# First pair's k ahead of q and turned in two halves, double score steps from the start, and a new order of all tasks

## The chip, the cores and the metric

The kernel runs on one core of a Trainium2 chip. The metric is the device time of one execution in microseconds (us); smaller is better. "Faster" and "slower" mean by more than 0.3% here, which is about what a measurement of this kernel can tell from no change.

The engines are TensorE (PE; its weight loads are shown apart as PEld), VectorE (DVE), ScalarE (ACT), GpSimd (POOL) and SyncE (SP, which only issues DMAs). DMAs are also issued by ACT and by POOL.

## The reference

A thresholded attention of 8 batches with 8 heads, 576 rows and head size 64, and behind it a mixer over all heads of a batch:

```
scores = q @ k.T / 8                                # 576 x 576 for each head
thresh = max(scores, axis=-1) - tau                 # tau = 0.02
scores = where(scores >= thresh, scores, -1e9)
attn   = softmax(scores)
x      = attn @ v                                   # heads side by side: 576 x 512 for each batch
u      = x + ((x.T @ U) @ V).T                      # rank 32
out    = u + relu(u @ w_ch1) @ w_ch2                # 512 -> 2048 -> 512
```

## The kernel before

**Pairs, steps and tiles.** Two heads of a batch make a pair: 32 pairs, numbered 0 to 31. 576 rows are four and a half times 128, so two neighbouring pairs share a tile: for them there are nine steps of 128 rows (four of each pair's own, one in which each pair has half of the rows), 144 steps in all, counted from 0 below. Each step has two score tiles of 128x576, one for each head.

**One pair on its way.** `load_tasks` brings q and k from HBM into `qkraw` (two buffers, pair p uses buffer p % 2) in eight DMAs: for each of the two heads, q and k, and the lower and the upper 64 partitions. `prepare_tasks` turns them on PE against an identity matrix (L568: four 128x128 turns for q and four for k, L581: one for the ninth tile of both) and ACT copies the results from PSUM to `qkT` (L574, L587). `score_tasks` multiplies q and k (L637, 16 matmuls for a step, in fp32) into the PSUM tiles `trio0` and `trio1`. Then, for each score tile, DVE scales, negates and takes the row minimum (`weigh`, L666), ACT computes the threshold of a step (L682) and the exponential (L689), and DVE selects and sums (`select`, L696, into `w_ring`). The weights are turned by DMA (L720) or, for some tiles of the first eight pairs, by PE and ACT (`turn_pe` L727, `copy_w` L737). `value_tasks` multiplies with v (L796, L804, later L800), normalises, and does the low-rank part; `mixer_tasks` does the two big products of a finished batch (L994 and L1010, L1027).

**Single and double steps.** A score task does one step or two at once. A double task holds both steps' scores in PSUM, so DVE has four tiles to weigh before PE must come again. The switch `LONE = 2` makes every step of pairs 0 and 1 single; from pair 2 on the first of nine is single and the other eight are done as four doubles. The next score task waits for the weighs of the two steps before it.

**The order is a table.** All work is cut into tasks. `ORDER` lists their numbers in the order in which they are emitted, found by a search ahead of time; each engine runs its own instructions in that order, and so does each DMA queue. A negative entry -n puts a filler matmul on zeros there (L469), which computes nothing and keeps PE at work; the table has 49 of them, all in the first part. `BANK` says which PSUM bank a task uses.

**Rings.** `w_ring` has four buffers: step n writes buffer n % 4, and its `select` must wait until the weights of step n - 4 have been turned.

## Time and profile before

| | us |
|---|---|
| median of 3 runs (590.59 to 592.37) | 591.26 |
| the profiled execution, its own time | 590.78 |
| its span, from the first to the last instruction | 589.0 |
| PE busy in the span | 568.7 |
| DVE busy | 509.9 |
| ACT busy | 460.2 |
| POOL busy | 331.7 |

The profiled execution is 0.48 us below the median and 1.78 us longer than its span. Busy time of PE counts fillers, and matmuls overlap, so that a PE with 9.95 us busy in 10 us has no gap. The granted clock of TensorE reads 1.00, its upper level of 2.4 GHz, in every stretch of the profile.

### The profile page before, as it was taken

The numbers are of one execution on the slowest core, as the hardware profiler recorded it, in microseconds if no ns is written. First come the engines' busy times: TensorE is split into PE (matmuls) and PEld (weight loads), VectorE is DVE, ScalarE is ACT, GpSimd is POOL, SyncE is SP. The second block draws the span as 40 slices with busy tenths as digits, with TensorE's granted clock in tenths as the row PEclk, the third lists the DMA queues.
The fourth block names the chain that finished last, engine by engine and source line by source line (L and its number), as shares of the span: only waits on it lengthen the run. The fifth ranks groups of instructions, "written<-read, shape, count | busy, mean of one in ns | idle before, by whom it ended". The sixth has DMA issues, their size and how long they took to land.

```text
span 589.0 us, 16929 instructions
## 1 busy us (share of the span) xinstructions
PE 568.7 (97%) x6142; PEld 345.8 (59%) x6214; DVE 509.9 (87%) x1400; ACT 460.2 (78%) x959; POOL 331.7 (56%) x580
## 2 busy tenths in 40 slices
PE   9898899999999999999999999999999999999996
PEld 3456655765666665555566665655665746556553
DVE  4999999999999999999998999999899799953101
ACT  4688999998899977998788987799877896774430
POOL 3887775968576748764666765566645551341000
PEclk9999999999999999999999999999999999999999
DMA  5999999969999999998989989999898798672303
GB/s 134 170 166 182 179 133 175 188 113 176 193 155 186 147 173 203 165 175 166 159 166 173 188 147 198 162 188 186 142 175 165 122 167 168 134 117 46 72 1 90
DMA packets 226996, 90.49 MB, mean 154 GB/s; under 512 B 205408, under 2 KB 217520, under 8 KB 226912
## 3 DMA queue, kind: packets, MB, share of 16 engines
q1 hardware_dynamic: 212544, 67.48, 70.5%
q0 software_dynamic: 13408, 21.58, 19.8%
q8 instruction: 49, 0.80, 0.6%
q10 hardware_dynamic: 960, 0.34, 0.2%
q14 instruction: 35, 0.29, 0.2%
HBM read 37.90 MB, written 9.44 MB: 80 GB/s over the span
## 4 chain that ended last, share of the span: by engine, by line
PE 56%; DVE 2%; issue 1%; ACT 0%
PE trio L637 13%; PE bank L1027 12%; PE trio L994 6%; PE bank L994 6%; PE trio L1027 4%; PE bank L800 4%; PE trio L800 3%; PE bank L1010 1%; PE bank L568 1%; PE trio L568 1%; DVE s_sb L666 1%; PE bank L875 1%; DVE w_ring L696 1%; PE bank L796 0%; PE trio L1010 0%
## 5 line engine op out<-in xcount | busy, mean ns | idle before, releaser
L689 ACT ACTIVATE e_sb<-s_sb,m 128x576 bf16<-128x576 f32 x288 | 217.5, 774 | 37.2 <-DVE s_sb L666 18.0
L696 DVE SCALAR_TENSOR_TENSOR w_ring<-s_sb,thr,e_sb 128x576 bf16<-128x576 f32 x288 | 229.7, 823 | 5.5 <-issue 1.5
L666 DVE TENSOR_SCALAR_CACHE_REDUCE s_sb<-trio 128x576 f32<-128x576 f32 x288 | 205.3, 749 | 9.3 <-PE trio L637 8.5
L637 PE MATMUL trio<-qkT 64*64 64x288 f32 (+2 forms) x2304 | 161.8, 410 | 2.1 <-DVE s_sb L666 1.6
L714 POOL COPY w_ring<-w_ring 128x128 bf16<-128x128 bf16 (+1 forms) x168 | 65.0, 395 | 115.3 <-DVE w_ring L696 71.7
L637 PEld LDWEIGHTS trio<-qkT 64*64 64x64 f32 x2304 | 81.4, 133 | 52.9 <-DVE s_sb L666 6.4
L1027 PE MATMUL bank<-W2b,R 128*128 128x512 bf16 x402 | 101.6, 380 | 1.9 <-issue 0.6
L506 POOL DMA_DIRECT2D qkraw<-in_k_dram x117 | 76.6, 656 | 25.9 <-PE trio L568 12.0
L1027 PEld LDWEIGHTS <-R 128*128 128x128 bf16 x576 | 53.1, 98 | 60.8 <-issue 9.1
L506 POOL DMA_DIRECT2D qkraw<-in_q_dram x117 | 76.4, 655 | 12.0 <-PE bank L581 3.0
L994 PEld LDWEIGHTS <-W1b 128*128 128x128 bf16 x512 | 46.7, 98 | 55.9 <-issue 10.9
L862 POOL TENSOR_TENSOR x<-x,rec 128x256 f32<-128x256 f32 (+1 forms) x84 | 52.7, 631 | 33.0 <-DVE x L855 21.8
L984 ACT ACTIVATE R<-bank 128x512 bf16<-128x512 f32 x80 | 47.2, 594 | 29.6 <-PE bank L994 16.4
L994 PE MATMUL bank<-uT,W1b 128*128 128x512 bf16 x244 | 66.6, 380 | 1.8 <-DVE x L855 0.2
L603 POOL TENSOR_TENSOR vh<-vraw_ring,vh 64x128 bf16<-64x128 f32 x64 | 53.5, 835 | 19.1 <-ACT vh L596 9.5
L800 PEld LDWEIGHTS <-wT_ring 128*128 128x128 bf16 x896 | 55.5, 98 | 9.9 <-issue 3.6
L994 PE MATMUL trio<-uT,W1b 128*128 128x512 bf16 x231 | 57.6, 379 | 0.4
L984 ACT ACTIVATE R<-trio 128x512 bf16<-128x512 f32 x64 | 37.5, 597 | 8.4 <-PE trio L994 8.0
L682 ACT ACTIVATE thr<-m,tau_t 128x2 f32<-128x2 f32 x144 | 41.5, 293 | 2.3 <-DVE s_sb L666 1.9
L1039 DVE TENSOR_TENSOR o<-bank,x 128x512 f32<-128x512 f32 x27 | 18.5, 686 | 27.5 <-PE bank L1027 27.2
L800 PE MATMUL bank<-vh,wT_ring 128*128 128x128 bf16 x496 | 35.6, 220 | 0.1
L1027 PE MATMUL trio<-W2b,R 128*128 128x512 bf16 x140 | 33.5, 379 | 0.3
(105 smaller groups left out, 719.6 us busy)
## 6 DMA issues: line engine op xcount, KB each, us to landing
out_dram<-o SPq DMA_DIRECT2D x71, 128.0 KB, 2.9
vraw_ring<-in_v_dram SPq DMA_DIRECT2D x32, 160.0 KB, 4.0
qkraw<-in_k_dram POOLq DMA_DIRECT2D x59, 80.0 KB, 4.2
qkraw<-in_q_dram POOLq DMA_DIRECT2D x58, 80.0 KB, 4.5
vraw_ring<-in_v_dram SPq DMA_DIRECT2D x32, 128.0 KB, 4.1
qkraw<-in_q_dram POOLq DMA_DIRECT2D x59, 64.0 KB, 4.2
qkraw<-in_k_dram POOLq DMA_DIRECT2D x58, 64.0 KB, 4.3
W1b<-in_moe_w_ch_dram POOLq DMA_DIRECT2D x8, 256.0 KB, 5.5
```

Of the source, the lines that this page charges most:

```text
L506: queue.dma_start(pr.qkraw[part, to, j, :], src[:, j, of, :])
L603: nc.gpsimd.tensor_tensor(out=pr.vh[part, tiles_, :, h, :], in0=raw[part, tiles_], in1=pr.vh[part, tiles_, :, 0, :], op=ALU.subtract)
L637: mm = nc.tensor.matmul(cols[part, lo:hi], a.tT[hs, 0, rows], a.tT[hs, 1, lo:hi], start=True, stop=True)
L666: nc.vector.tensor_scalar(out=s_sb, in0=score_cols(slot, x), scalar1=-scale, scalar2=None, op0=ALU.mult, op1=ALU.min, accum_out=m[:, x:x + 1])
L689: nc.scalar.activation(out=e_sb, in_=s_sb, func=ACT.Exp, bias=m[:, x:x + 1], scale=-1.0)
L696: nc.vector.scalar_tensor_tensor(out=w_sb[:, 0:S], in0=s_sb, scalar=thr_[:, x:x + 1], in1=e_sb, op0=ALU.is_le, op1=ALU.mult, accum_out=pr. ...
L714: nc.gpsimd.tensor_copy(out=w_sb[:, xs, S:640], in_=w_sb[:, xs, 512:S])
L800: nc.tensor.matmul(av[:, 2 * a + j, :], w, pr.vh[:, kt, j, :, :], start=kt == 0, stop=False)
L862: nc.gpsimd.tensor_tensor(out=x, in0=x, in1=over_sum(part), op=ALU.mult)
L984: nc.scalar.activation(out=R2[:, fts, lo:hi], in_=bank[t.got[0]].rearrange("p (f c) -> p f c", c=hi - lo), func=ACT.Relu)
L994: nc.tensor.matmul(bank[t.got[0]], W1b[:, dt, ft * P:(ft + 1) * P], bt.uT[:, dt, :], start=(dt == 0), stop=(dt == 3))
L1027: nc.tensor.matmul(ch, R2[:, ft, lo:lo + P], W2b[:, ft, :], start=(ft == 0), stop=(ft == 15))
```

## The change

- `LONE = 0`: of every nine steps, the first pair's too, only the first is single. The 144 steps are now 16 single and 64 double tasks, where they were 24 single and 60 double.
- Pair 0 gets loads and turns of its own. k comes first on SP and ACT; its lower 64 partitions (`kA`, four turns of 64 columns) and its upper ones (five turns, with k's ninth tile) are turned apart, and DVE copies the first half while ACT copies the second in two instructions. q's first tile (`q0`) is loaded apart by two DMAs on POOL, turned apart and copied by DVE. The first score step waits for these alone, and q's other tiles (`q`, `qk4`) are loaded, turned and copied afterwards.
- The identity matrix is made by a task of its own, behind the two q0 loads on POOL.
- `ORDER` and `BANK` are searched anew for all 3289 tasks (3284 before). The number of fillers is 49 as before.

```diff
-LONE = 2
+LONE = 0
...
 ORDER = (
-    24, 22, 21, 26, 20, 23, 19, 25, 29, 42, 43, 28, 46, 27, -3, -3, -3, -3, -3, -3, -3, -3, -3, -3, -3, -3, -3, -3, 30, 39, 34, 31, 32,
...
         freed = [got("q", p - 2), got("k", p - 2), got("qk4", p - 2), got("q0", p - 2), got("kA", p - 2)]
...
+        def tile0(part, t):
+            def load(_):
+                nc.gpsimd.dma_start(pr.qkraw[part, 0, :, :], qv[:, :, t, :])
+
+            loads["q0"].append(add(POOL, 0.655, load, [], dma=0.2))
+
+        if p == 0:
+            for j, e in enumerate((SP, SCA)):
+                loads["k"].append(one("k", e, lo, slice(5, 9), slice(0, 4), j, []))
+                loads["k4"].append(one("k", e, hi, slice(4, 9), slice(4, 9), j, []))
+            tile0(lo, 0)
+            tile0(hi, 5)
+            for j in range(2):
+                t = one("q", SP, lo, slice(1, 5), slice(1, 5), j, [])
+                loads["q"].append(t)
+                loads["q4"].append(t)
+                loads["q"].append(one("q", POOL, hi, slice(1, 4), slice(6, 9), j, []))
...
+    def first_turns(pr, loads):
+
+        def turn(cost, part, ins, deps):
+            rows = part.stop - part.start
+
+            def turned(t):
+                for at, i in enumerate(ins):
+                    nc.tensor.transpose(bank[t.got[0]][:, at * rows:(at + 1) * rows], pr.qkraw[part, i, :, :],
+                                        ident[part, part])
+
+            return add(PE, cost, turned, [done["ident"]] + deps, banks=1, kind="qk")
...
+        full, lo, hi = slice(0, P), slice(0, HB), slice(HB, P)
+        t = done["kA", 0] = turn(0.36, lo, (5, 6, 7, 8), loads["k"])
+        done["kAT", 0] = copied(0.335, t, 1, 0, 4, P, e=VEC)
+        t = done["k", 0] = turn(0.44, hi, (4, 5, 6, 7, 8), loads["k4"])
+        done["k4T", 0] = copied(0.12, t, 1, 512, 1, HB, last=False)
+        done["kT", 0] = copied(0.26, t, 1, HB, 4, P, at=HB, after=done["k4T", 0])
+        t = done["q0", 0] = turn(0.15, full, (0,), loads["q0"])
+        done["q0T", 0] = copied(0.2, t, 0, 0, 2, HB, e=VEC)
+        t = done["q", 0] = turn(0.33, full, (1, 2, 3), loads["q"])
+        done["qT", 0] = copied(0.37, t, 0, P, 6, HB)
+        t = done["qk4", 0] = turn(0.08, lo, (4,), loads["q4"])
+        done["qk4T", 0] = copied(0.12, t, 0, 512, 1, HB)
...
         deps = [got(name, p + a) for p, i in steps for a in range(2 if i == 4 else 1)
-                for name in ("qT", "kT", "qk4T")]
+                for name in ("qT", "kT", "qk4T")
+                if p + a or i == 4 or name == "kT" or i and name == "qT"]
+        deps += [got(name, p) for p, i in steps for name in ("q0T", "k4T", "kAT") if not p]
```

**PE at the start.** These are PE's instructions from the end of the opening fillers to the first score step; `qkraw0` is pair 0's q and k as loaded, `qkT0` the turned ones. Before, behind 14 fillers:

```order
L568 MATMUL trio1_160<-ident_60,qkraw0_103 128x128 [waits DMAHW2_49,DMAHW1_49,DMAHW3_49,DMASW0_49,Pool_49]
L568 MATMUL trio1_160<-ident_60,qkraw0_103 128x128 x3
L581 MATMUL trio0_159<-ident_60,qkraw0_103 128x128 [waits DMAHW0_49,DMASW1_49]
L568 MATMUL bank7_162<-ident_60,qkraw0_103 128x128 [waits DMAHW6_49,DMAHW4_49]
L568 MATMUL bank7_162<-ident_60,qkraw0_103 128x128 x3
L469 LDWEIGHTS zeros_58
L469 MATMUL trio0_159<-zeros_58 128x512
...
L637 MATMUL trio0_159<-qkT0_105 64x288 [waits Activation_49]
```

Now, behind 10 fillers:

```order
L595 MATMUL bank6_156<-ident_60,qkraw0_98 128x64 [waits DMAHW1_49,DMAHW0_49,Pool_49]
L595 MATMUL bank6_156<-ident_60,qkraw0_98 128x64 x3
L595 MATMUL trio1_155<-ident_60,qkraw0_98 128x64 [waits DMAHW4_49,DMAHW2_49]
L595 MATMUL trio1_155<-ident_60,qkraw0_98 128x64 x4
L595 MATMUL trio0_154<-ident_60,qkraw0_98 128x128 [waits DMASW1_49,DMASW0_49]
L468 LDWEIGHTS zeros_58
L468 MATMUL trio1_155<-zeros_58 128x512
L708 MATMUL trio0_154<-qkT0_100 64x288 [waits DVE_49,Activation_49]
```

Ten turns stand ahead of the first scores where nine stood, nine of them of 64 columns, behind four fillers fewer; q's other tiles have moved behind the first score step.

**PE at the turns of pair 2** (in `qkraw0` again). Before, q and k of pair 2 are turned apart, among the single steps 4 to 6, and the weights of step 1 (`w_ring1`) are turned on PE ahead of step 4. These are the rows from the end of that turning, over step 4's scores and the first turns, to the second turns, which stand between steps 5 and 6:

```order
L727 LDWEIGHTS w_ring1_81 [waits Pool_49]
L727 MATMUL bank7_162<-identb_65,w_ring1_81 128x128
L637 MATMUL trio0_159<-qkT0_105 64x288 [waits DVE_49]
L637 MATMUL trio0_159<-qkT1_106 64x288 [waits Activation_49]
...
L568 MATMUL bank6_161<-ident_60,qkraw0_103 128x128 [waits DMAHW5_49,DMAHW2_49,DMAHW0_49]
L568 MATMUL bank6_161<-ident_60,qkraw0_103 128x128 x3
...
L568 MATMUL trio0_159<-ident_60,qkraw0_103 128x128 [waits DMAHW6_49,DMAHW7_49,DMAHW3_49,DMAHW1_49]
L568 MATMUL trio0_159<-ident_60,qkraw0_103 128x128 x3
```

Now both stand together between the double tasks of steps 5 and 6 and of steps 7 and 8, and the turning of step 1's weights stands behind the latter:

```order
L637 MATMUL bank7_157<-ident_60,qkraw0_98 128x128 [waits DMAHW5_49,DMAHW7_49,DMAHW4_49,DMAHW3_49]
L637 MATMUL bank7_157<-ident_60,qkraw0_98 128x128 x3
L637 MATMUL bank6_156<-ident_60,qkraw0_98 128x128 [waits DMAHW2_49,DMAHW3_49,DMAHW1_49,DMAHW0_49]
L637 MATMUL bank6_156<-ident_60,qkraw0_98 128x128 x3
L708 MATMUL trio0_154<-qkT1_101 64x288 [waits DVE_49]
L708 MATMUL trio0_154<-qkT1_101 64x288
...
L650 MATMUL bank6_156<-ident_60,qkraw0_98 128x128 [waits Activation_49]
L800 LDWEIGHTS w_ring1_76
L800 MATMUL bank7_157<-identb_61,w_ring1_76 128x128
```

Everything behind the turns on PE, steps 7 and 8 first, now waits for all eight loads of pair 2.

**SP's queue** holds pair 2's loads. Now its 18th DMA is the first turning of weights, and the last of the eight loads that those turns wait for is its 26th:

```order
L505 DMA qkraw0_98<-in_k_dram 64x4x64 [waits DMAHW3_49,PE_49]
L793 DMA_TRANSPOSE wT_ring0_79<-w_ring0_75 128x10x128 [waits DMAHW4_49,Pool_49]
L505 DMA qkraw0_98<-in_k_dram 64x5x64 [waits DMAHW5_49,PE_49]
L547 DMA vraw_ring1_84<-in_v_dram 64x2x64 [waits DMAHW6_49]
L505 DMA qkraw0_98<-in_k_dram 64x5x64 [waits DMAHW7_49]
L505 DMA qkraw0_98<-in_q_dram 64x4x64 [waits DMASW3_49,DMAHW0_49,DMASW0_49,PE_49]
L505 DMA qkraw0_98<-in_q_dram 64x5x64 [waits DMAHW1_49,DMASW1_49,PE_49]
L505 DMA qkraw0_98<-in_q_dram 64x5x64 [waits DMAHW2_49]
L505 DMA qkraw0_98<-in_q_dram 64x4x64 [waits DMAHW3_49,DMASW2_49]
L505 DMA qkraw0_98<-in_k_dram 64x4x64 [waits DMAHW4_49]
```

Before, that turning was the 24th, and one load of pair 2 stood behind it:

```order
L506 DMA qkraw0_103<-in_k_dram 64x4x64 [waits DMAHW0_49]
L506 DMA qkraw0_103<-in_q_dram 64x5x64 [waits DMAHW1_49]
L720 DMA_TRANSPOSE wT_ring0_84<-w_ring0_80 128x10x128 [waits DMAHW2_49,Pool_49]
L506 DMA qkraw0_103<-in_q_dram 64x5x64 [waits DMAHW3_49]
L530 DMA vraw_ring0_88<-in_v_dram 64x2x64 [waits DMAHW4_49,Activation_49]
```

Seven loads of pair 2 now stand behind the first turning of weights, and that turning stands six places further ahead.

What the two orders hold ahead of the 25th step (step 24):

| ahead of step 24's scores on PE | before | now |
|---|---|---|
| fillers | 49 | 49 |
| steps (single tasks, double tasks) | 23 (11, 6) | 23 (3, 10) |
| tasks that turn q and k | 21 | 22 |
| turns of weights, products with v, low-rank products, spreads, turns of u | 13, 12, 4, 5, 3 | 13, 12, 4, 4, 3 |
| **ahead of step 24's first weigh on DVE** | | |
| weighs, selects | 48, 44 | 48, 43 |
| normalisings, sums, inverses | 12, 4, 4 | 12, 4, 4 |
| copies of pair 0's turns | 0 | 2 |

## Rows read from the trace of the kernel before

**Rows 1.** Stretches: us; busy PE, PEld, DVE, ACT, POOL; PEclk; DMA; GB/s

```profile
0.00:9.60 9.60, 8.25 (x42) 3.63 (x43) 2.25 (x12) 2.73 (x5) 2.11 (x8) 1.00 0.57 131
9.60:70.00 60.40, 51.99 (x750) 32.51 (x750) 58.71 (x165) 49.26 (x99) 46.17 (x87) 1.00 1.13 170
70.00:90.00 20.00, 19.20 (x258) 12.06 (x261) 19.48 (x56) 19.87 (x41) 14.80 (x25) 1.00 1.07 147
90.00:520.00 430.00, 425.28 (x4677) 263.38 (x4731) 413.65 (x1141) 362.46 (x765) 263.15 (x452) 1.00 0.98 166
```

**Rows 2.** DVE's groups, 9.6 to 90 us: busy, mean ns, idle before them

```profile
L827 DVE TENSOR_TENSOR x<-bank,rec 128x256 f32<-128x256 f32 x8 | 3.3, 416 | 0.0
```

**Rows 3.** Timeline of the start: start, duration (us), instructions, idle before and releaser

```profile
0.74 2.38 SPq L506 DMA_DIRECT2D qkraw<-in_q_dram  x3
...
0.99 5.50 PE L469 MATMUL trio<-zeros 128*128 128x512 bf16 x14 [0.99 <-DVE tau_t L397]
...
6.33 0.61 PE L568 MATMUL trio<-ident,qkraw 128*128 128x128 f32 x4
...
6.89 0.60 PE L568 MATMUL bank<-ident,qkraw 128*128 128x128 f32 x4
...
7.62 0.60 ACT L574 COPY qkT<-bank 128x512 f32<-128x512 f32 x1
8.27 1.20 PE L637 MATMUL trio<-qkT 64*64 64x288 f32 x16 [0.36 <-ACT qkT L574]
...
9.61 0.76 DVE L666 TENSOR_SCALAR_CACHE_REDUCE s_sb<-trio 128x576 f32<-128x576 f32 x1 [6.28 <-PE trio L637]
```

**Rows 4.** Timeline of PE's weight loads, the last of the opening fillers

```profile
5.24 0.15 PEld L469 LDWEIGHTS <-zeros 128*128 128x128 bf16 x1 [0.27 <-issue]
5.66 0.34 PEld L469 LDWEIGHTS <-zeros 128*128 128x128 bf16 x2 [0.27 <-issue]
```

**Rows 5.** Timeline of DVE, 9 to 30 us and at step 24

```profile
11.42 0.82 DVE L696 SCALAR_TENSOR_TENSOR w_ring<-s_sb,thr,e_sb 128x576 bf16<-128x576 f32 x1 [0.36 <-ACT thr L682]
...
14.35 0.81 DVE L696 SCALAR_TENSOR_TENSOR w_ring<-s_sb,thr,e_sb 128x576 bf16<-128x576 f32 x1
...
15.09 0.75 DVE L666 TENSOR_SCALAR_CACHE_REDUCE s_sb<-trio 128x576 f32<-128x576 f32 x1
...
15.77 0.75 DVE L666 TENSOR_SCALAR_CACHE_REDUCE s_sb<-trio 128x576 f32<-128x576 f32 x1
...
27.12 0.76 DVE L666 TENSOR_SCALAR_CACHE_REDUCE s_sb<-trio 128x576 f32<-128x576 f32 x1 [0.69 <-PE trio L637]
...
85.20 0.74 DVE L666 TENSOR_SCALAR_CACHE_REDUCE s_sb<-trio 128x576 f32<-128x576 f32 x1
```

**Rows 6.** ACT's groups, whole run: busy, mean ns, idle before them

```profile
L574 ACT COPY qkT<-bank 128x512 f32<-128x512 f32 x33 | 19.2, 584 | 3.7 <-PE bank L568 3.5
...
L587 ACT COPY qkT<-trio 128x128 f32<-128x128 f32 x22 | 5.8, 266 | 2.5 <-PE trio L581 2.4
```

**Rows 7.** Loads of pair 0's q and k (issued 0.5 to 2.6 us), issue to landing

```profile
DMA to landing us min/median/max: 2.7/3.5/3.8
```

**Rows 8.** DMAs issued from 13 to 20 us: KB each, median us to landing

```profile
qkraw<-in_k_dram SPq DMA_DIRECT2D x2, 80.0 KB, 2.8
qkraw<-in_q_dram SPq DMA_DIRECT2D x2, 80.0 KB, 5.3
...
wT_ring<-w_ring SPq DMA_TRANSPOSE x1, 7.0
```

**Rows 9.** Timeline of SP's queue

```profile
12.51 1.27 SPq L506 DMA_DIRECT2D qkraw<-in_k_dram  x2
...
16.55 2.30 SPq L720 DMA_TRANSPOSE wT_ring<-w_ring  x1
```

**Rows 10.** Timeline of PE at pair 2's second turns

```profile
24.25 0.63 PE L568 MATMUL trio<-ident,qkraw 128*128 128x128 f32 x4 [0.78 <-issue]
...
25.88 1.20 PE L637 MATMUL trio<-qkT 64*64 64x288 f32 x16
```

More of the change, by code (lines that the diff above doesn't have):

```diff
@@ L558, in phase, with identities, unit, unit_b @@
         order.phase = sum(p >= n for n in PHASES)
+    def identities():
+        def unit(_):
+            make_identity(nc, ident)
+        t = add(POOL, 0.85, unit, [])
+        def unit_b(_):
+            nc.vector.tensor_copy(out=identb, in_=ident)
+        done["ident"], done["identb",] = t, add(VEC, 0.1, unit_b, [t])
+    def first_turns(pr, loads):
[6 more added lines that the diff above has]
+            return add(PE, cost, turned, [done["ident"]] + deps, banks=1, kind="qk")
+        def copied(cost, t, x, lo, n, step, at=0, e=SCA, last=True, after=None):
+            def copy(_):
+                fn = nc.scalar.copy if e == SCA else nc.vector.tensor_copy
+                to = pr.tT[:, x, lo:lo + HB] if n == 1 else \
+                    pr.tT[:, x, lo // P * P:lo // P * P + n * step].rearrange("p (n c) -> p n c", c=step)
+                if n > 1:
+                    to = to[:, :, lo % P:lo % P + HB] if step == P else to
+                fn(out=to, in_=bank[t.got[0]][:, at:at + n * HB].rearrange("p (n c) -> p n c", c=HB)
+                   if n > 1 else bank[t.got[0]][:, at:at + HB])
+            return add(e, cost, copy, [t, after], frees=[t] if last else [])
+        full, lo, hi = slice(0, P), slice(0, HB), slice(HB, P)
[10 more added lines that the diff above has]
+        done["qk4T", 0] = copied(0.12, t, 0, 512, 1, HB)
     def prepare_tasks(p):
@@ L564, in prepare_tasks @@
         before = [got("S", p - 2, 3), got("S", p - 2, 4)]
+        if p == 0:
+            first_turns(pr, loads)
+            values_tasks(p, pr, loads)
+            return
         for x, (name, t0) in enumerate((("q", 0), ("k", 5))):
@@ L592, in prepare_tasks, with values_tasks @@
                               frees=[task])
+        values_tasks(p, pr, loads)
+    def values_tasks(p, pr, loads):
         def high(_):
@@ L732, in step_tasks @@
             if i < 4 and (x == 1 and p < EARLY and i >= 1 or p == NPAIR - 1 and i == 3):
-                t = done["wT", tiles[0]] = add(PE, 0.28, turn_pe, [twin_] + free, banks=1,
+                t = done["wT", tiles[0]] = add(PE, 0.28, turn_pe, [twin_, got("identb")] + free, banks=1,
                                                kind="wT")
@@ L1111 @@
     weight_loads()
+    identities()
     for p in range(0, NP, 2):
```

12 lines of the change are left out of this document (5 added, 7 removed), and 388 rows, old and new, of tables (BANK, ORDER).

## The prediction

> **What bounds the kernel now.** I read the busy times by stretch first [rows 1]. From 90 to 520 us PE is busy for 425.28 of 430 us: PE is the bound there, and what any other engine does costs only what reaches PE. From 9.6 to 70 us it is otherwise: DVE is busy for 58.71 of 60.40 us, idle for 1.69, while PE has 51.99 with fillers in it. From 70 to 90 us both are nearly full (19.48 and 19.20 of 20 us), and ACT too (19.87). So the run has three parts: a head until DVE's first weigh at 9.61 us [rows 3], a part in which DVE sets the pace, and one in which PE does. The hand-over lies at about step 24, whose first weigh starts at 85.20 us [rows 5]. The end is then: DVE's first weigh, plus DVE's work and waits up to step 24, plus PE's work behind step 24. The change can move each of the three.
>
> In the head the reader is to see the chain: 14 fillers from 0.99 us, turns from 6.33 to 7.49 us (6.89 + 0.60), ACT's last copy from 7.62 to 8.22 us, the scores from 8.27 us, the weigh at 9.61 us, 1.34 us behind the start of its scores [rows 3]. In DVE's part there are two plain waits: 0.36 us for the first threshold and 0.69 us for PE at 27.12 us [rows 5]; the other 0.64 of the 1.69 us is in smaller pieces.
>
> **Work moved over the hand-over.** The table of the two orders shows what stands ahead of step 24. On PE it is the same 49 fillers and 23 steps, and nearly the same rest. On DVE, counted from the first weigh (the two new copies stand ahead of that), there is one select less, 0.74 us (14.35 to 15.09) [rows 5]. For that, PE has one spread and the turning of four tiles of a later pair left to do behind step 24: four turns are 0.45 us at 0.11 us each (five from 6.33 to 6.89) [rows 3], and the spread, four matmuls, is taken at half of that, 0.2. These two sums cancel: 0.74 gained, 0.65 given back, **0.1 us gained**. Pair 0's own pieces and the single steps that became double are work of PE in a part where PE waits; nothing is due for them. Cover gone, a 64-column turn more would cost 0.11 us.
>
> **The head.** The opening fillers stand 0.42 us apart (5.24 to 5.66) [rows 4]; ten from 0.99 us end at 5.24 us. The loads then needed: k's lower half is issued first on SP and ACT, at 0.74 us, and landed at most 3.8 us later [rows 3, 7], by 4.5 us; the upper half is second in both queues, issued by 1.6 us (three issues in 2.38 us), landed by 5.4 us; q0's is the second of POOL's two, issued by 2.3 us at SP's pace, landed by 6.1 us. All of them come just in time for their turns, so these begin at 5.24 us. Nine turns (k) at 0.11 us and a pipe of 0.2 us give 6.4 us. Then ACT copies 64 and 256 columns; 512 take 0.584 us and 128 take 0.266 [rows 6], so I take 0.25 + 0.40 = 0.65 and arrive at 7.1 us. DVE's two copies (0.42 us for 256 columns [rows 2], and less) run beside it. Scores then start at 7.15 us, **1.1 us ahead**.
>
> The uncertain part is the pace of these turns. The granted clock reads 1.00 of 2.4 GHz in the first 9.6 us as everywhere [rows 1], but the fillers' spacing of 0.42 us for 512 columns is that of 1.2 GHz, and three of them (the 12th to the 14th) then take 0.67 us from 5.66 us to the first turn at 6.33 [rows 3, 4], so that the spacing halves at about 5.7 us. Turns that begin at 5.24 us run two at the lower pace, 0.2 us more: I take **0.9 us** for the head. If all ten ran at the lower pace, they would take 1.0 us more and 0.1 us would be left; with none slow and short copies 1.3 us. The Trainium skill (TensorE: Matmul & The Clock Gate, Part 1: The HAM clock gate) says that the lower clock is the default, that activity of PE releases it, and that the moment varies from run to run. By that rule fewer fillers buy no time of their own, since turns that come before the release run at half the pace; the spacing of the fillers in this trace agrees that the release falls inside the opening. The sum by the rule, if the release came after the last turn, is the 0.1 us of the rival below.
>
> **DVE's waits.** The first threshold's 0.36 us stays: weigh, ACT, select are in the same chain. The 0.69 us at 27.12 us goes. It arose because single step 6 started at 25.88 us, behind pair 2's second turns at 24.25 us, which waited [rows 10]. With doubles, DVE has two selects (1.48 us) between a task's last weigh and the next one's first, and PE needs 1.34 us from start to weigh [rows 3], so in itself a double hides its scores with 0.14 us to spare.
>
> But the same turns, now all eight together, stand ahead of steps 7 and 8 and wait for SP's 26th DMA. The 18th place was reached at 12.51 us [rows 9]; the turning of weights there needs step 0's second select, which by the head above ends at about 11.9 us, and POOL's copy behind it, so it issues at about 12.5 us and holds the queue for 2.30 us. Seven more issues at 0.64 us (two in 1.27) put the 26th at 19.3 us. Loads issued at that time landed after 2.8 us (k) or 5.3 us (q) [rows 8]: 22.1 or 24.6 us. I take the later, of the loads issued last in that stretch. Eight turns (0.9 us) and 1.34 us make the first weigh of step 7 possible at 26.85 us. DVE gets there with 14 weighs (0.68 us, 15.09 to 15.77) and 10 selects [rows 5]: 16.9 us behind its first weigh at 8.7 us, with the 0.36 us and 0.1 us more, 26.05 us. It waits **0.8 us** (0 with the early landing). Queued behind on PE is the turning of step 1's weights, for which step 5's first select waits to have `w_ring1` free: scores of two steps from 25.5 us (twice 1.05), one turn and five matmuls end at about 28.3 us, and DVE is there at 26.85 + 1.36 = 28.2 us: **0.1 us** (0 to 0.5).
>
> So DVE's waits were 1.69 and will be 0.36 + 0.8 + 0.1 + 0.64 = 1.9 us, **0.2 us lost**. Sum: 0.9 + 0.1 - 0.2 = 0.8 us off the profiled execution's 590.78, so 590.0 us for one like it. Its span of 589.0 becomes 588.2, with the same 1.78 us around it. That execution is 0.48 us below the median of the runs shown; for the median I forecast 591.26 - 0.8, **590.4 us**. Everything behind 90 us is in a new order too. PE's 4.72 us without work there [rows 1] can grow or shrink by about 1 us; I take no difference.
>
> **Rivals.** *The new order keeps what the head gains and takes DVE's waits away.* The loads of pair 2 land after 2.8 us, no wait stands ahead of step 7, and of 1.69 us of idle time only the 0.36 stays: 1.3 + 0.1 + 1.3 = 2.7 us, 588.6 us. For it: DVE alone sets the pace there, so each gap closed counts in full. Against it: the DMA share is 1.13 in that stretch [rows 1], so loads queue.
>
> *The head start doesn't come.* All ten turns run at the lower pace, scores start at 8.15 us, and the gain of 0.1 us less 0.2 us leaves nothing: 591.3 us. Against it: the spacing halved at 5.7 us under fillers just as dense.
>
> *Slower: pair 2's turns block PE.* If the 26th DMA takes a little longer than the turning of weights did (7.0 us [rows 8]), say 8 us, it lands at 27.3 us. Then step 7's weigh comes at 29.5, 3.5 us late, and step 5's select behind the turning of `w_ring1` another 0.5 us. DVE's waits are 0.36 + 3.5 + 0.5 + 0.64 = 5.0 us, 3.3 more than before; less 1.0 us of head and moved work that is 2.3 us lost, 593.5 us. It is slower by over 0.3% (1.8 us) from a landing at 26.8 us, 7.5 us behind the issue. For it: those loads stand behind a turning of weights, POOL loads pair 3 at the same time, and the DMAs are full there. Against it: q's loads, issued in the middle of the same crowd, took 5.3 us [rows 8]. The Trainium skill (Trainium Kernel Development and Optimization, Key Constraints) says that the queues of SP, ACT and POOL run on the same 16 DMA engines and interleave, so that spreading loads over queues only saves issue time. That speaks for this rival: what POOL loads early for pair 3 delays pair 2 on SP. The trace agrees as far as a load that took 2.7 to 3.8 us in the opening [rows 7] took 5.3 us in the crowd [rows 8]; no row shows what one queue alone would do.
>
> **Numbers.** Chances: 0.41 for the forecast, 0.08 for the missing head start, 0.36 for the larger gain, 0.15 for the blocked PE. The forecast's own range is 589.3 to 591.3 us. The range for 8 in 10 takes in most of the larger gain and the near part of the slower case: 587.7 to 592.9 us. Faster by over 0.3% (below 589.5 us; this is about what a measurement can tell from no change) 0.37, within it 0.48, slower 0.15.
>
> **What would show it.** The first score matmul at 7.0 to 7.5 us and the first weigh at about 8.7 us show the head right. The weigh of step 7 is to wait about 0.8 us for PE, at about 26 us, behind turns that wait for `qkraw`; no wait there means the larger gain, over 3 us the slower case. Step 24's first weigh is to start at about 84.2 us. If that holds and the end doesn't follow, the later part of the order is what I had wrong: then PE's idle time from 90 to 520 us differs from 4.7 us by what is missing.

## The result and the profile after

The changed kernel is slower: 594.10 us median (591.46 to 598.58, 19 runs) beside 590.87 us for the kernel before on the same chip (589.66 to 594.03, 19 runs), a ratio of 1.0059 with a 95% interval of 1.0043 to 1.0076, 3.5 us. The forecast was 590.4 us with a range up to 592.9. The profiled execution took 592.78 us (span 591.0), 1.3 us less than the median, so it is one of the milder ones. Line numbers: in the changed kernel, turns of pairs are L637 (before L568), scores L708 (L637), weighs L739 (L666), selects L769 (L696), fillers L468 (L469).

The head's numbers came as forecast. PE's timeline of the changed kernel (start, us, line, tiles, form, count):

```profile
3.52 1.91 PE L468 MATMUL trio<-zeros 128*128 128x512 bf16 x4
5.37 0.37 PE L595 MATMUL bank<-ident,qkraw 64*128 64x64 f32 x1
...
5.53 0.31 PE L595 MATMUL bank<-ident,qkraw 64*128 64x64 f32 x1
...
5.64 0.31 PE L595 MATMUL bank<-ident,qkraw 64*128 64x64 f32 x1
...
7.06 1.20 PE L708 MATMUL trio<-qkT 64*64 64x288 f32 x16
```

and DVE's, over the first weigh and the wait for the first threshold:

```profile
8.41 0.76 DVE L739 TENSOR_SCALAR_CACHE_REDUCE s_sb<-trio 128x576 f32<-128x576 f32 x1 [1.50 <-PE trio L708]
...
10.22 0.82 DVE L769 SCALAR_TENSOR_TENSOR w_ring<-s_sb,thr,e_sb 128x576 bf16<-128x576 f32 x1 [0.36 <-ACT thr L755]
```

Scores start at 7.06 us (8.27 before) and the first weigh at 8.41 us (9.61), 1.2 us earlier [rows 3]. Then come pair 2's loads. SP's queue:

```profile
13.15 1.50 SPq L793 DMA_TRANSPOSE wT_ring<-w_ring  x1
14.76 0.65 SPq L505 DMA_DIRECT2D qkraw<-in_k_dram  x1
15.46 0.61 SPq L547 DMA_DIRECT2D vraw_ring<-in_v_dram  x1
16.12 0.60 SPq L505 DMA_DIRECT2D qkraw<-in_k_dram  x1
16.89 3.26 SPq L505 DMA_DIRECT2D qkraw<-in_q_dram  x4
20.20 0.61 SPq L505 DMA_DIRECT2D qkraw<-in_k_dram  x1
```

and that last one among the DMA issues (KB, us to landing):

```profile
qkraw<-in_k_dram SPq DMA_DIRECT2D x1, 64.0 KB, 5.5
```

It is issued at 20.20 us and lands at 25.7 us. PE stands for it, with the scores of steps 7 and 8 behind it, though these need only pair 1:

```profile
22.14 0.60 PE L468 MATMUL bank<-zeros 128*128 128x512 bf16 x2
25.82 1.07 PE L637 MATMUL bank<-ident,qkraw 128*128 128x128 f32 x8 [3.07 <-issue]
26.81 2.17 PE L708 MATMUL trio<-qkT 64*64 64x288 f32 x32
...
32.06 0.70 PE L708 MATMUL trio<-qkT 64*64 64x288 f32 x4 [1.68 <-ACT wT_ring L810]
```

DVE's timeline there, and at the first weigh of step 24:

```profile
28.43 0.76 DVE L739 TENSOR_SCALAR_CACHE_REDUCE s_sb<-trio 128x576 f32<-128x576 f32 x1 [1.15 <-PE trio L708]
...
84.68 0.75 DVE L739 TENSOR_SCALAR_CACHE_REDUCE s_sb<-trio 128x576 f32<-128x576 f32 x1
```

PE is idle for 3.07 us and again for 1.68 us, DVE waits 1.15 us, and step 24 comes at 84.68 us: 0.5 us earlier than before (85.20), where 1.0 was forecast. The end doesn't follow. From that weigh to the end of the span it takes 506.3 us (591.0 - 84.68), and 503.8 us before (589.0 - 85.20), with a granted clock of 1.00 from 84.6 to 589 us in both traces. So this execution, 2.0 us slower than that of the kernel before, loses its time behind step 24. The windows (busy us of PE, PEld, DVE, ACT, POOL; granted clock; DMA share; GB/s) show what [rows 1] has nowhere:

```profile
30.00:32.00 2.00, 0.38 (x5) 0.20 (x5) 2.00 (x5) 2.00 (x6) 2.00 (x4) 1.00 0.80 175
32.00:34.00 2.00, 1.79 (x16) 0.60 (x16) 2.00 (x7) 1.24 (x4) 1.24 (x4) 1.00 0.42 114
34.00:36.00 2.00, 2.00 (x13) 1.74 (x9) 2.00 (x7) 2.00 (x5) 1.55 (x3) 0.56 1.13 241
36.00:38.00 2.00, 1.96 (x21) 0.94 (x23) 1.97 (x8) 1.98 (x6) 1.41 (x3) 0.59 0.79 107
38.00:40.00 2.00, 1.73 (x41) 1.02 (x33) 1.55 (x6) 0.54 (x1) 1.86 (x3) 1.00 1.03 240
```

From 34 to 38 us most of the stretch runs at the lower level, 1.2 GHz. Over the 19 runs the mean granted clock (0.994 on average, 0.999 for the kernel before) falls with the time: a line through them rises by 0.58 us for each 0.001, correlation 0.85. Further on there are two new stalls of PE, one behind DVE's finish of a mixer's output, one behind ACT's relu between the mixer's two products:

```profile
285.67 0.44 PE L948 MATMUL bank<-xb_ring,Ub 128*128 128x128 bf16 x5 [0.85 <-DVE o L1112]
...
522.61 1.02 PE L1100 MATMUL trio<-W2b,R 128*128 128x512 bf16 x4 [0.69 <-ACT R L1057]
```

In the kernel before no idle time of PE behind step 24 is longer than 0.31 us. So there were three suspects: the late loads, the lower clock behind PE's waits, and the later order.

### The profile page after: what moved, and what is told of

Read it like the earlier page. It is cut to its first block, busy times and chain, and to the rows that moved or that the text cites. A ratio compares the mean times of both kernels' runs of the same rounds, so it can differ in the third digit from the quotient of the medians.

```text
span 591.0 us, 17017 instructions
## 1 busy us (share of the span) xinstructions
PE 573.8 (97%) x6219; PEld 346.0 (59%) x6219; DVE 514.7 (87%) x1402; ACT 463.0 (78%) x960; POOL 322.5 (55%) x582
## 4 chain that ended last, share of the span: by engine, by line
PE 47%; DVE 3%; ACT 1%; DMA 1%; POOL 1%; issue 0%; DVEq 0%; ACTq 0%; POOLq 0%
PE bank L1100 10%; PE trio L708 10%; PE trio L1067 6%; PE bank L1067 5%; PE trio L1100 4%; PE bank L873 3%; PE trio L873 3%; PE trio L637 1%; PE bank L1083 1%; DMA wT_ring<-w_ring 1%; DVE w_ring L769 1%; DVE s_sb L739 1%; ACT e_sb L762 1%; PE bank L948 1%; PE bank L637 1%; PE trio L1083 1%
## 5 line engine op out<-in xcount | busy, mean ns | idle before, releaser
L769 DVE SCALAR_TENSOR_TENSOR w_ring<-s_sb,thr,e_sb 128x576 bf16<-128x576 f32 x288 | 231.3, 829 | 8.5 <-ACT thr L755 4.0
L739 DVE TENSOR_SCALAR_CACHE_REDUCE s_sb<-trio 128x576 f32<-128x576 f32 x288 | 204.8, 749 | 6.9 <-PE trio L708 5.5
L708 PE MATMUL trio<-qkT 64*64 64x288 f32 (+2 forms) x2304 | 160.7, 411 | 2.8 <-ACT wT_ring L810 1.7
L787 POOL COPY w_ring<-w_ring 128x128 bf16<-128x128 bf16 (+1 forms) x168 | 56.8, 348 | 128.0 <-DVE w_ring L769 101.0
L708 PEld LDWEIGHTS trio<-qkT 64*64 64x64 f32 x2304 | 81.8, 133 | 55.9 <-issue 7.8
L1100 PE MATMUL bank<-W2b,R 128*128 128x512 bf16 x448 | 108.9, 379 | 0.3 <-ACT R L1057 0.3
L1067 PE MATMUL bank<-uT,W1b 128*128 128x512 bf16 x284 | 71.4, 380 | 0.1
L935 POOL TENSOR_TENSOR x<-x,rec 128x256 f32<-128x256 f32 (+1 forms) x84 | 50.1, 604 | 37.7 <-DVE x L928 28.6
L1057 ACT ACTIVATE R<-bank 128x512 bf16<-128x512 f32 x82 | 48.8, 597 | 22.2 <-PE bank L1083 12.9
L873 PE MATMUL bank<-vh,wT_ring 128*128 128x128 bf16 x576 | 41.2, 219 | 0.3 <-ACT wT_ring L810 0.2
L1057 ACT ACTIVATE R<-trio 128x512 bf16<-128x512 f32 x62 | 35.9, 597 | 7.1 <-PE trio L1067 4.3
L1100 PE MATMUL trio<-W2b,R 128*128 128x512 bf16 x128 | 30.7, 379 | 0.7 <-ACT R L1057 0.7
```

The lines of the kernel that those rows point to most:

```text
L708: mm = nc.tensor.matmul(cols[part, lo:hi], a.tT[hs, 0, rows], a.tT[hs, 1, lo:hi], start=True, stop=True)
L739: nc.vector.tensor_scalar(out=s_sb, in0=score_cols(slot, x), scalar1=-scale, scalar2=None, op0=ALU.mult, op1=ALU.min, accum_out=m[:, x:x + 1])
L769: nc.vector.scalar_tensor_tensor(out=w_sb[:, 0:S], in0=s_sb, scalar=thr_[:, x:x + 1], in1=e_sb, op0=ALU.is_le, op1=ALU.mult, accum_out=pr. ...
L787: nc.gpsimd.tensor_copy(out=w_sb[:, xs, S:640], in_=w_sb[:, xs, 512:S])
L873: nc.tensor.matmul(av[:, 2 * a + j, :], w, pr.vh[:, kt, j, :, :], start=kt == 0, stop=False)
L935: nc.gpsimd.tensor_tensor(out=x, in0=x, in1=over_sum(part), op=ALU.mult)
```

## The experiments

The experiments edit `ORDER` alone, apart from the "head" kernels, which also set `LONE` and the banks. Task numbers: 216 and 214 are pair 2's turns, 217 and 215 their copies, 126 the scores of steps 5 and 6, 148 those of steps 7 and 8, 243 those of step 9; 203 to 210 SP's loads of pair 2; 223 to 229 POOL's loads of pair 3; 77 the first turning of weights, 58 a load of v; -8 and -7 fillers. Longer tables shift line numbers by 6 or 7; those of the head kernels are 22 lower.

**Filling PE's idle times.**

```diff
# fill_first
-    132, -8, -8, 216,
+    132, -8, -8, -8, -8, -8, -8, -8, -8, -8, -8, -8, -8, -8, -8, 216,
# fill_second
-    141, 243,
+    141, -7, -7, -7, -7, -7, -7, 243,
# fill_both: both
```

> The changed kernel with 12 more fillers (some 0.22 us each, 2.6 us) on PE in the 3.07 us in which it waits for pair 2's loads; nothing else changes. Theory (the clock): the idle of PE there makes the granted clock fall a few us later, by a length that differs from run to run; the runs of the changed kernel lie on a line of 591.5 us at a mean clock of 1.000 plus 0.58 us for each 0.001 below. Then the mean clock comes back to 0.999 to 1.000 and the median to about 591.5 us. Rival 1 (late loads and the order): DVE's wait of 1.15 us and the later order cost the time, the clock only goes along; then the median stays at 594 us. Rival 2 (the second idle): the 1.68 us at 32.06 us alone brings the clock down; then the median stays at 594 us here, and the next kernel repairs it.

> The changed kernel with 6 fillers (1.3 us) in the second idle of PE, 1.68 us ahead of 32.06 us, and the first idle of 3.07 us left as it is. Theory (the clock, by the first idle): the clock still falls, median 594 us. Rival 2 (the second idle alone): clock 1.000, 591.5 us. Both idles needed together for the fall: also 591.5 us. Rival 1 (late loads and the order): 594 us, at a lower clock or not.

> Both idles of PE filled, 12 and 6 fillers. The clock theory in either form: clock 1.000 in every run, spread of the runs as narrow as that of the kernel before, median 591.5 us or a little below, with DVE's wait of 1.15 us for step 7 still there. Rival 1 (late loads and the order): 594 us.

Measured: fill_first 593.29 us, ratio 1.0027 [1.0006, 1.0048], mean clock 0.997; fill_second 594.69, 1.0045 [1.0027, 1.0063], 0.995; fill_both 593.79, 1.0049 [1.0027, 1.0072], 0.9985. With both idle times filled the clock is that of the kernel before, and the time is not. The clock as main cause falls. A share of it is not excluded: fill_first's ratio is 0.0032 below that of the changed kernel, and the two intervals overlap only just. The profiles of fill_second and fill_both differ in an instructive way. fill_second, PE and then DVE:

```profile
25.47 1.88 PE L644 MATMUL bank<-ident,qkraw 128*128 128x128 f32 x8 [2.91 <-DMA qkraw<-in_q_dram]
27.28 2.97 PE L715 MATMUL trio<-qkT 64*64 64x288 f32 x32
```

```profile
29.71 0.76 DVE L746 TENSOR_SCALAR_CACHE_REDUCE s_sb<-trio 128x576 f32<-128x576 f32 x1 [3.30 <-PE trio L715]
```

fill_both, DVE:

```profile
28.84 0.76 DVE L746 TENSOR_SCALAR_CACHE_REDUCE s_sb<-trio 128x576 f32<-128x576 f32 x1 [2.15 <-PE trio L715]
```

DVE's wait for steps 7 and 8 is 3.30, 2.15 and in fill_first 2.87 us: the 1.15 us of the changed kernel's own profile was a mild case, since there DVE itself came late, behind a select of 1.95 us (shown at the end). In fill_second the clock fell at once (0.50 from 26 to 28 us), the turns and scores ran at half pace, and from the start of the turns to the weigh it took 4.24 us; in the changed kernel it took 2.61 us (25.82 to 28.43). Where the lower clock meets the wait, it adds 1.6 us to it.

**Scores ahead of the turns.**

```diff
# scores_first
-    -8, -8, 216, 137, 214, 217, 136, 130, 109, 148, 224, 110, 122, 65, 230, 215, 120, 88, 143,
+    -8, -8, 137, 136, 130, 109, 148, 216, 214, 224, 110, 122, 217, 65, 230, 120, 88, 215, 143,
```

> The changed kernel with the scores of steps 7 and 8 ahead of pair 2's eight turns on PE (their two copies on ACT behind them): these scores need pair 1 only. No filler is added. DVE's wait of 1.15 us goes whatever the clock does. PE's idle behind the two fillers at 22.7 us shrinks to about 1.7 us (until DVE has weighed steps 5 and 6). The clock theory: clock near 1.000, 591.5 - 1.1 = 590.4 us. Rival 1 (late loads): 594.1 - 1.1 = 593.0 us or, if the whole loss came from PE blocked by these loads, 590.4 us with no link to the clock. If the idle that is left still brings the clock down, 591 to 593 us with a mean clock below 0.998.

Measured: 593.60 us, 1.0037 [1.0021, 1.0054], mean clock 0.994. The weighs of steps 7 and 8 wait for nothing, and the next thing in PE's queue is late instead, the turning of `w_ring1` (L806), for which a select waits:

```profile
31.48 0.82 DVE L775 SCALAR_TENSOR_TENSOR w_ring<-s_sb,thr,e_sb 128x576 bf16<-128x576 f32 x1 [3.44 <-PE trio L806]
```

The wait moved by one place and did not shrink.

**Loads earlier.**

```diff
# loads_first
-    46, 86, 77, ..., 83, 210, ..., 208, ..., 204, ..., 203, ..., 205, ..., 206, ..., 209,
+    46, 86, 210, 208, 204, 203, 205, 206, 209, 77, ..., 83,
# pool_later
-    228, 204, 99, 226, 203, 225, 205, 105, 227, ..., 229, ..., 223, ..., 2, ..., 148, 224,
+    204, 99, 203, 205, 105, ..., 2, ..., 148, 228, 226, 225, 227, 229, 223, 224,
# loads_pool: both
```

> The changed kernel with the seven loads of pair 2 that stand behind SP's first turning of weights moved ahead of it, and ahead of the v load among them; nothing else moves. In the changed kernel the last of these loads is issued at 20.2 us and lands near 26 us; here it is issued some 2.1 us earlier (1.5 us for the turning, 0.6 for v). Theory now (late loads): PE stands at pair 2's turns, DVE waits for steps 7 and 8 behind them (1.15, 2.87, 3.30 and 2.15 us in four profiled executions), and this is the loss; the clock only goes along. Then the wait here is 0 to 1 us, and the median 592 us. Rival (the clock is the loss): the shorter idle brings the clock back too, but the kernel with both idles filled had the clock and not the time, so this should stay at 593.5 us if late loads are not the cause. Rival (the later order): 594 us.

> The changed kernel with six of POOL's loads of pair 3 (issued from 16.2 to 24 us) moved behind POOL's casts of Vb, so that they don't run beside SP's loads of pair 2. If POOL's loads delay those of SP on the shared DMA engines: SP's last load of pair 2 lands 1 to 2 us earlier, DVE waits 1 us less, median 593 us or a little below. If SP's own queue with its turning of weights sets the landing: no earlier landing, 594 us. If pair 3's loads then come too late for their turns at 34 us: slower, 595 us.

> Both moves together. Late loads theory: the last load of pair 2 lands ahead of 23 us, no wait of DVE for steps 7 and 8, mean clock 0.999 or 1.000, and the prediction's larger gain: 0.9 us of the head reach the end, median 590.5 us, below the kernel before by 0.5 to 1 us. Rival (the later order costs about 1.5 us behind the hand-over): 592 us with no wait in DVE's part.

Measured: loads_first 592.38 us, 1.0016 [0.9997, 1.0034]; pool_later 593.04, 1.0026 [1.0007, 1.0045]; loads_pool 591.62, 1.0002 [0.9984, 1.0020]. Their last load of pair 2 lands at 21.3, 23.6 and 20.5 us, and no weigh of DVE waits for PE there by more than 0.2 us. loads_pool on PE:

```profile
22.16 0.60 PE L474 MATMUL bank<-zeros 128*128 128x512 bf16 x2
22.60 1.04 PE L643 MATMUL bank<-ident,qkraw 128*128 128x128 f32 x8
```

The turns follow the fillers at once. With the loads moved, the ratio falls from 1.0059 to 1.0002, and that with the mean clock still at 0.995: most of the loss is gone and the clock is not back. Each move alone gives back a part; with POOL's loads of another pair out of the way, the same load on SP lands some 2 us earlier. pool_later changes one thing more: POOL's casts come earlier, and no select is stretched beside them (at the end). That DVE gains this only where no load makes it wait is argued, not tested.

**The loss added to the kernel before.** Its last load of pair 2 (198) is put behind three more DMAs of SP (two loads of v and a turning), and in late_fill fillers go into the wait.

```diff
# late_before
-    198, 87, 53, 208, ..., 76, ..., 49,
+    87, 53, 208, ..., 76, ..., 49, 198,
# late_fill: the same, and
-    114, 209,
+    114, -3, -3, -3, -3, -3, -3, -3, -3, -3, -3, -3, -3, -3, -3, -3, -3, 209,
```

> The kernel before with one DMA moved: the last load of pair 2 stands on SP behind the next two turnings' first and a load of v, 2.9 us later (issued near 21.8 us instead of 18.9). Its landing then is about 26.5 us instead of 24.15, PE stands at pair 2's second turns for 3 us instead of 0.78, DVE waits 3 us instead of 0.69. Theory (late loads): 591.3 + 2.0 to 2.5 = 593.5 us, the loss of the change, without its head, its double steps or its later order, and a mean clock below that of before. Rival (late loads are not the cause): 591.3 us.

> The kernel before with its load of pair 2 late (595.1 us, ratio 1.0046) and 16 more fillers (3.5 us) on PE in the 3.7 us in which it stands for it. There the turns behind the wait ran at the lower clock, and DVE's wait was 5.26 us, 2.4 us from the turns' start to the weigh more than at full pace would be 1.6. If the clock costs time of its own where such a wait lies on DVE's way: 1.3 to 1.6 us less, ratio 1.002. If it only goes along: ratio 1.0046 again, with a mean clock back at 0.9985.

Measured: late_before 595.14 us, 1.0046 [1.0027, 1.0065], mean clock 0.997; late_fill 594.70, 1.0055 [1.0032, 1.0078], 0.9986. late_before on PE (L574 turns, L475 fillers, L643 scores) and on DVE:

```profile
27.63 0.77 PE L574 MATMUL trio<-ident,qkraw 128*128 128x128 f32 x4 [3.74 <-issue]
28.20 2.34 PE L475 MATMUL trio<-zeros 128*128 128x512 bf16 x5
30.47 1.63 PE L643 MATMUL trio<-qkT 64*64 64x288 f32 x16
```

```profile
32.14 0.76 DVE L672 TENSOR_SCALAR_CACHE_REDUCE s_sb<-trio 128x576 f32<-128x576 f32 x1 [5.26 <-PE trio L643]
```

One DMA moved in the old order costs as much as the whole change: a late load is enough for such a loss, without the new head, the double steps or the later order. The delay is larger than the change's own, though (DVE waits 5.26 us here, at most 3.3 us there), so this doesn't show that the late loads are all of the change's loss. The five fillers behind the turns took 2.34 us; the kernel before has them at full pace:

```profile
24.71 1.24 PE L469 MATMUL trio<-zeros 128*128 128x512 bf16 x5
```

In late_fill the clock stayed up; DVE's wait:

```profile
31.24 0.76 DVE L673 TENSOR_SCALAR_CACHE_REDUCE s_sb<-trio 128x576 f32<-128x576 f32 x1 [4.66 <-PE trio L644]
```

From the turns' start to this weigh it is 2.87 us instead of 4.51, but the load landed 0.7 us later, and the median did not move. That fillers repay what the clock takes is thus shown in place, by 1.6 us, and not in the time of a run.

**The head alone, in the old order.**

```diff
# head_alone: before's ORDER with single steps, pair 0's tasks from the change
-LONE = 0
+LONE = 2
# head_early: the same, and the last load of pair 1 (53) forward
-    50, 213, 69, 57, 70, 72, 214, ..., 56, 73, 74, 53,
+    50, 53, 213, 69, 57, 70, 72, 214, ..., 56, 73, 74,
# head_best: also SP's loads of pair 2 behind 53, POOL's 233, 230, 3, 0 behind its casts
-    50, 53, 213, 69, 57, 70, 72, 214,
+    50, 53, 213, 214, 212, 210, 208, 211, 209, 207, 69, 57, 70, 72,
```

> The kernel before with the head of the changed one alone: pair 0 loaded and turned as in the change, the fillers ahead of the first turns 10, and from the second step on the order of before, with its single steps, on the same banks. The head term: first weigh 1.2 us earlier, all of it reaching the end if nothing comes late: median 591.3 - 1.2 = 590.1 us. If pair 2's loads set the pace here too (SP's queue is no faster than before): DVE waits longer for steps 5 and 6 and the gain is gone, 591.3 us. Slower than 591.3 us would mean that the head itself harms something.

> The kernel with the head alone, but the last load of pair 1 issued ahead of the first of pair 2 (near 10.5 us instead of 13.1). There it landed at 18.0 us, 4.9 us behind its issue, and PE stood 4.2 us for it; here it lands near 13 us and that wait goes. Pair 2's last load still lands near 24 us, as in the kernel before, so by the theory (loads set the pace up to 26 us) DVE reaches it 1.2 us earlier and waits for it: 590.8 to 591.3 us. If the head's 1.2 us reach the end: 590.1 us. If the head itself harms: 593 us or more.

> The kernel with the head alone and pair 1's last load early (ratio 0.9992, PE waits 1.59 us at 21.4 us for a load of pair 2, DVE 1.54 us at 24.0), with all eight loads of pair 2 on SP ahead of pair 1's v and of the first turning of weights, and POOL's loads of W1, U and the first two of pair 3 behind its casts. By the theory of late loads these land ahead of 19 us, both waits go, and the head's lead of 1.2 us reaches the end: ratio 0.997 to 0.998, 590.0 us. If pair 1's v then comes too late for its product: no gain, ratio 0.999 or more.

Measured: head_alone 594.54 us, 1.0067 [1.0042, 1.0091]; head_early 592.03, 0.9992 [0.9973, 1.0012]; head_best 594.98, 1.0054 [1.0034, 1.0075]. In head_alone pair 1's last load is issued at 13.14 us and needs 4.9 us, where the kernel before issues it at 12.51 us and it needs 2.6. PE (L615 turns) stands for it, and DVE behind PE:

```profile
18.26 1.09 PE L615 MATMUL bank<-ident,qkraw 128*128 128x128 f32 x4 [4.21 <-DMA qkraw<-in_q_dram]
```

```profile
23.01 0.76 DVE L717 TENSOR_SCALAR_CACHE_REDUCE s_sb<-trio 128x576 f32<-128x576 f32 x1 [5.76 <-PE trio L686]
```

With that load forward the loss is gone, but no gain can be measured: DVE now reaches pair 2's loads earlier and waits 1.54 us for them. The first weigh starts at 7.88 us, 1.7 us earlier than before, and that of step 7 at 29.71 us, only 0.25 us earlier (29.96): the lead is spent in the wait. With those loads forward too (head_best) others are late, the turned weights and pair 3's q:

```profile
26.55 0.82 DVE L747 SCALAR_TENSOR_TENSOR w_ring<-s_sb,thr,e_sb 128x576 bf16<-128x576 f32 x1 [2.78 <-DMA wT_ring<-w_ring]
...
38.53 0.82 DVE L747 SCALAR_TENSOR_TENSOR w_ring<-s_sb,thr,e_sb 128x576 bf16<-128x576 f32 x1 [2.35 <-PE bank L778]
```

In head_best the DMA share is 1.18 to 1.32 from 20 to 38 us, and in each of these three orders something is late.

**More opening fillers, with late loads and with early ones.**

```diff
# head_late (changed kernel), pool_late (pool_fill, below)
-    20, 52, 28, 49, -3, -3, -3, -3, -3, -3, -3, -3, -3, -3, 34,
+    20, 52, 28, 49, -3, -3, -3, -3, -3, -3, -3, -3, -3, -3, -3, -3, -3, -3, -3, 34,
```

> The changed kernel with 15 instead of 10 fillers ahead of the first turns, so that the scores start some 1.1 to 1.2 us later, as in the kernel before; the loads and all else stay. If late loads set the pace (pair 2's last load lands near 26 us whatever the head does), DVE waits 1.1 us less for steps 7 and 8 and the time stays: 594 us, as with the early head. If the head's lead reaches the end: 595.3 us.

> The kernel with both moves of loads and 6 fillers in the second idle (0.9989 of the kernel before), with 15 instead of 10 opening fillers. There nothing waits for loads, so the head's 1.1 to 1.2 us reach the end: ratio 0.9989 + 0.0019 = 1.0008, some 592.1 us beside 590.9. If the head is worth nothing here either, another wait of 1.2 us has to be gone in its place: ratio 0.999.

Measured: head_late 593.59 us, 1.0039 [1.0014, 1.0064], beside 1.0059 for the changed kernel; pool_late 594.51 us, 1.0038 [1.0011, 1.0064], against 0.9989 for pool_fill. The five fillers were to take the lead of 1.2 us away and took little of it. In head_late's trace the scores start at 7.26 us and the first weigh at 8.62 us (7.06 and 8.41 in the changed kernel), since the turns behind the longer row of fillers run at twice the pace (below, "The head"). In pool_late the first weigh starts at 8.96 us instead of 8.30 us. So head_late doesn't test what the lead is worth. The 2.9 us between pool_late and pool_fill are more than the delay of 0.7 us that their profiles show; each ratio is uncertain by about 0.0025, 1.5 us. What the lead is worth stays open in both.

**Towards a version without late loads.**

```diff
# pool_fill: loads_pool, and
-    141, 243,
+    141, -7, -7, -7, -7, -7, -7, 243,
# all_three: pool_fill, and the finish 1264 ahead of two selects
-    1800, ..., 1802, ..., 1894, ..., 1264,
+    1264, 1800, ..., 1802, ..., 1894,
# pool_v: pool_later, the fillers, 1264 as above, and v behind the loads
-    58, 87, 63, 62, 208, ..., 209,
+    87, 63, 62, 208, ..., 209, 58,
```

> The kernel with both moves of loads (591.6 us, mean clock 0.995 over its runs) with 6 more fillers on PE in the idle of 1.73 us ahead of step 9's scores, behind which its clock fell from 30 to 38 us. With the loads early this is the only idle of PE over 1 us before 90 us. If the clock costs time of its own: mean clock 0.999 to 1.000, DVE's waits at 36 and 38 us (0.75 and 0.90 us) gone, median 590.5 us. If the clock only goes along, as with the late loads: clock up, time the same, 591.6 us.

> As the kernel with both moves and the 6 fillers, and on DVE one finish of the mixer moved ahead of two selects: in every execution of the new order so far PE stood 0.85 us at 284 to 286 us, because the bank of its next low rank is freed by that finish. If this stall is the later order's cost: 0.7 to 0.85 us off the kernel with fillers, 589.8 us. If DVE, busy for 34.7 of 35 us there, is as much the bound as PE: no change against it.

> The changed kernel with POOL's six loads of pair 3 behind its casts, as in the kernel whose profile showed no wait of DVE over 0.6 us (ratio 1.0026, landing at 23.6 us), and besides: on SP only the small load of v (0.7 us) moved behind pair 2's last load, the first turning of weights left ahead of them, the 6 fillers in the second idle, and the mixer's finish ahead of two selects. By the theory of late loads the last load lands near 23 us, 0.7 us earlier than there, which leaves a margin where that kernel had none, and the turnings of weights stay early, so that nothing is late behind them: ratio 0.998, 590.0 to 590.5 us. If the DMA engines are simply full, something else is late instead, as with all loads ahead of the turnings: ratio 0.999 to 1.002.

Measured: pool_fill 590.93 us, 0.9989 [0.9965, 1.0013], mean clock 0.9987; all_three 591.40, 0.9989 [0.9971, 1.0007]; pool_v 590.74 beside 591.89 for the kernel before, 0.9981 [0.9965, 0.9998]. In all_three PE's stall at 285 us is gone and the time is the same. The later order has a price all the same. all_three's trace reaches step 24 at

```profile
82.52 0.75 DVE L746 TENSOR_SCALAR_CACHE_REDUCE s_sb<-trio 128x576 f32<-128x576 f32 x1
```

2.7 us earlier than the kernel before, and its span of 588.4 us is only 0.6 us shorter. From step 24's first weigh to the end the 13 traces with the new order take 505.6 to 507.4 us, the six with the old one 503.8 to 505.1, on average 1.8 us less. PE's stall of 0.69 us at 522 us is in all thirteen and in none of the six; with the other stall taken away that part is no shorter (505.9 us in all_three, 505.7 in pool_fill). No run joins the new first part with the old later order, so what else makes up the price is open.

pool_v's ratio lies below 1, by 1.1 us; that is less than the 0.3% that counts as faster here. Its profile is of its slowest executions but one (592.35 us, clock 0.995) and still has the wait, with the scores at half pace behind it:

```profile
24.34 1.30 PE L644 MATMUL bank<-ident,qkraw 128*128 128x128 f32 x8 [1.85 <-DMA qkraw<-in_k_dram]
25.57 3.59 PE L715 MATMUL trio<-qkT 64*64 64x288 f32 x32
```

```profile
28.55 0.76 DVE L746 TENSOR_SCALAR_CACHE_REDUCE s_sb<-trio 128x576 f32<-128x576 f32 x1 [2.58 <-PE trio L715]
```

The load (19.66 us) lands at 24.3 us here. Six of its twelve executions had a clock of 1.000 and took 589.4 to 591.0 us; whether the load came in time in them was not seen. Nor do these runs tell the share of each of its four edits.

## Why the forecast was wrong

**The head** came out right in its number (1.2 us, for 0.9 taken and 1.3 as the upper bound), and in part by luck. A turn of 64 columns was priced at 0.11 us, with two turns at the lower pace. In this trace the turns of a bank stand 0.11 us apart (5.53, 5.64), but in head_late, where they come later, 0.06 to 0.07 us:

```profile
6.10 0.22 PE L602 MATMUL bank<-ident,qkraw 64*128 64x64 f32 x1
...
6.17 0.22 PE L602 MATMUL bank<-ident,qkraw 64*128 64x64 f32 x1
...
6.23 0.22 PE L602 MATMUL bank<-ident,qkraw 64*128 64x64 f32 x1
```

So nearly all turns of the changed kernel ran at half pace, which the prediction feared. It didn't show, since a turn costs half of what was taken and the turns of two banks run side by side. In the fourteen traces with the new head and ten fillers the first weigh starts at 7.80 to 8.49 us.

**The step that failed** is two terms of the sum.

One is the work behind step 24, in a new order too: "I take no difference". The prediction's own sign for it came true: step 24 came near its forecast (84.68 us for 84.2) and the end didn't follow. Of the 2.8 us by which the profiled execution missed the 590.0 us forecast for one like it, 0.5 lie ahead of step 24 and 2.3 behind it; there 506.3 us stand against 503.8 before, and work moved over the hand-over accounts for 0.65 of these 2.5. The idle time of 4.72 us that PE was said to have is a misreading: the trace before lacks matmul records. It holds 4677 from 90 to 520 us, that of head_alone, in the same order there, 4740, and with these PE is busy for 429.05 of 430 us.

The other is the wait behind pair 2's turns: "It waits 0.8 us". The mechanism was the right one; its terms were too small. Step 7's weigh was put at 26.85 us and came at 28.43. The last load was issued 0.9 us later than taken (20.20 us for 19.3): the first turning of weights is SP's 19th DMA, not its 18th (five places ahead of before, not six), and the last load its 27th, which costs 0.65 us; the turning then held the queue for 1.6 us instead of 2.30, but the seven issues behind it took 5.4 us instead of 4.5. The load took 0.2 us more than the slowest of the rows (5.5 us for 5.3 [rows 8]), and 2.6 us passed from the turns' start to the weigh, for 0.9 + 1.34. In the changed kernel and the five others that issue this load at 20.1 to 20.8 us it landed at 25.4 to 26.4 us, 4.9 to 6.3 us behind its issue. And the wait was priced without the clock: up to 1.6 us more where it falls under the turns. Together the wait is 1.15 to 3.3 us in the executions seen, with the same wait at another instruction in scores_first (3.44). That is the slower rival, which had a chance of 0.15 and was to decide from a landing at 26.8 us; with the price behind step 24 on top, landings of 25.4 to 26.4 us were enough.

**The sum** added the head's 0.9 us to this wait as if both could be had. The wait was worked out from DVE's earlier arrival, so the arithmetic held, but it hid what head_early's trace shows: where a load whose landing doesn't move ends last, the head's lead makes DVE wait longer.

**The larger gain** (0.36) needed loads that land 2.8 us behind their issue. They do so when moved (loads_pool: 2.7 us). Then the ratio is 0.998 to 1.000, where that rival's 588.6 us would be 0.9955. In all_three's trace its 2.7 us do reach step 24; 2.1 of them are lost behind it.

**The rule on queues** in the prediction spoke for the rival. The trace of pool_later agrees with the Trainium skill (Trainium Kernel Development and Optimization, Key Constraints), by which queues of different engines share the same DMA engines: with six loads of POOL moved away, SP's last load took 3.8 us instead of 4.9 to 6.3.

**The clock.** The Trainium skill (TensorE: Matmul & The Clock Gate, Terms) prices throttled time at its length times the share of the clock taken away. An estimate by that page, with the mean clock of fill_both and of the changed kernel: 0.9985 - 0.9943 = 0.0042 of 591 us, 2.5 us of the 3.5 lost. The runs don't bear it out as a separate cost: fill_both and late_fill have their clock back (0.9985, 0.9986) and lose 0.5%, loads_pool has not (0.995) and loses nothing. Late loads make both the wait and the idle PE, which is the likely reason that time and clock go together over the runs. Shown is the price in one place, 1.6 us where slowed turns and scores lie on DVE's way.

**What is shown.** Moving the loads takes the loss away (1.0059 to 1.0002), and one DMA made late in the old order brings such a loss. That the later order's price keeps the gain from coming is read from the traces; no run isolates it. **Open** are the parts of that price, what share of the loss the clock has in a typical run (one trace per kernel shows one landing), and why pool_late lost 2.9 us.

## What to carry to other kernels

A lead in the head can be spent in the next wait: before crediting it, look for the next load whose landing doesn't move with it. A wait in a full DMA stretch is to be priced by issues and a landing slower than the slowest row of the stretch (here 6.3 us against 5.3), not by its median. Putting other work ahead of the instruction that stands is not enough by itself: in scores_first the wait moved to the next one. "No difference" for a part in a new order is a term to be checked: compare the time from the hand-over to the end as soon as there is a trace. A clock that falls along with the time need not be the cause: give the clock back, and see whether the time follows.
